# Attention in half sequences of 384 tokens, interleaved with the expert MLP, with zero-padded two-head matmuls

## The chip, the cores and the metric

The kernel runs on one core of a Trainium2 chip. Times are device microseconds (us), medians of several executions.

Engines: PE is the matmul array and PEld its weight loads, DVE the vector engine, ACT the scalar engine, POOL the GpSimd engine, SP the sync engine that issues loads and stores.

## The reference

Four batches, 8 heads, 768 tokens, head size 64. Attention is causal and linear, with a decay `lam` per head, and a running state per head. Its output is the input of an MLP with an ELU between two matmuls.

```python
for b in range(nb):                      # blocks of 64 tokens, in order
    intra = (qb @ kb.T * Dmask) @ vb     # Dmask = lam ** (i - j), causal
    inter = (qb * lam_pow) @ kv_state
    out[:, :, sl] = intra + inter
    kv_state = lam_block * kv_state + (kb * rev_pow).T @ vb
...
x = out.transpose(0, 2, 1, 3).reshape(3072, 512)
h = x @ w_in                             # 512 -> 2048
g = where(h > 0, h, exp(min(h, 0)) - 1)
return g @ w_out                         # 2048 -> 512
```

## The kernel before

It works in chunks of 128 tokens and pairs of heads. The whole attention comes first, then the whole MLP; the attention's buffers are closed in between. A head has 64 channels, so most attention matmuls use half of the 128x128 array: 64 rows (scores) or 64 columns (state update, output).

```python
def emit_A(gi, cp):                       # state update, scores, mask
    for dc in range(2):
        c = 2 * cp + dc
        for hh in range(2):
            ps = slice(hh * 64, (hh + 1) * 64)
            nc.tensor.matmul(psU[ps, c * 64 : (c + 1) * 64],
                lhsT=kd[:, hh, c, :], rhs=vn[:, hh, c, :], start=True, stop=True)
    ...
    nc.tensor.matmul(psSa[:, dc * 128 : (dc + 1) * 128],
        lhsT=qkt[0:64, c, 1, :], rhs=qkt[0:64, c, 0, :], start=True, stop=True)
    nc.tensor.matmul(psSb[:, dc * 128 : (dc + 1) * 128],
        lhsT=qkt[64:128, c, 1, :], rhs=qkt[64:128, c, 0, :], start=True, stop=True)
...
for si, (gi, cp) in enumerate(stages):    # attention, all of it
    ...
asb_cm.__exit__(None, None, None)
aps_cm.__exit__(None, None, None)
...
for mt in range(NMT):                     # then the MLP: 6 tiles of 512 tokens
    ...
    for n in range(NFT):                  # NFT = 16
        emit_mm1(n)                       # 4 matmuls of 512 columns, Exp, Relu, combine
        if n >= MLAG:
            emit_mm2(n - MLAG)            # 4 matmuls of 512 columns
    ...
    for ms in range(4):                   # eviction and store
        nc.vector.tensor_copy(osb[:], psM[ms][:])
```

Of the kernel before, what the change touches and what calls it, by code (L numbers as in the profile page):

```python
# [15 lines left out]
def kernel(  # L17
# [9 lines left out]
):  # L27
    nc = tc.nc
# [3 lines left out]
    NCH = S // L  # L32
    NST = NCH // 2
    NHP = H // 2
    NTOK = B * S
# [3 lines left out]
    MT = 512  # L39
    NMT = NTOK // MT  # L40
    MLAG = 3

    cpool = ctx.enter_context(tc.tile_pool(name="cst", bufs=1))
    xpool = ctx.enter_context(tc.tile_pool(name="xt", bufs=1))
    wpool = ctx.enter_context(tc.tile_pool(name="w", bufs=1))

    lam_b = cpool.tile([128, H], FP32, name="lam_b")
    nc.sync.dma_start(out=lam_b[:], in_=lam.unsqueeze(0).broadcast_to([128, H]))
    loglam = cpool.tile([128, H], FP32, name="loglam")
    nc.scalar.activation(loglam[:], lam_b[:], AF.Ln)  # L50

# [12 lines left out]
    caus2 = causT[:].unsqueeze(1).broadcast_to([128, 2, 128])  # L64

    iota_i = cpool.tile([128, 1], I32, name="iota_i")
    nc.gpsimd.iota(iota_i[:], pattern=[[0, 1]], base=0, channel_multiplier=1)
    in4 = cpool.tile([128, 4], FP32, name="in4")
    nc.vector.tensor_copy(in4[:, 0:1], iota_i[:])
    nc.vector.tensor_scalar_mul(in4[:, 1:2], in4[:, 0:1], -1.0)  # L70
    nc.vector.tensor_scalar(
        out=in4[:, 2:3], in0=in4[:, 0:1], scalar1=-1.0, scalar2=float(L),
        op0=ALU.mult, op1=ALU.add,
    )
    nc.vector.memset(in4[:, 3:4], float(L))
    pows = []
    for h in range(H):
        pw = cpool.tile([128, 4], FP32, name=f"pow{h}")
        nc.scalar.activation(pw[:], in4[:], AF.Exp, scale=loglam[:, h : h + 1])  # L79
        pows.append(pw)  # L80
    lamLp = cpool.tile([128, NHP], FP32, name="lamLp")
    for hp in range(NHP):
        h0, h1 = 2 * hp, 2 * hp + 1
        nc.vector.tensor_copy(lamLp[0:64, hp : hp + 1], pows[h0][0:64, 3:4])  # L84
        nc.vector.tensor_copy(lamLp[64:128, hp : hp + 1], pows[h1][64:128, 3:4])

    xt = [
        xpool.tile([128, NTOK], FP16, name=f"xt{hp}", tag=f"xt{hp}")
        for hp in range(NHP)
    ]  # L90

    w_in16 = [
        wpool.tile([128, DFF], FP16, name=f"wi16_{kk}", tag=f"wi16_{kk}")
        for kk in range(NHP)
    ]
    w_out16 = [
        wpool.tile([128, DM], FP16, name=f"wo16_{n}", tag=f"wo16_{n}")
        for n in range(NFT)
    ]
    w_jobs = [(w_in16[kk], moe_w_in[kk * 128 : (kk + 1) * 128, :]) for kk in range(NHP)]  # L100
    w_jobs += [(w_out16[n], moe_w_out[n * 128 : (n + 1) * 128, :]) for n in range(NFT)]
    w_sched = {}
    for j in range(NHP):
        w_sched[4 + 3 * j] = j
    for j in range(NFT):
        w_sched[15 + j] = NHP + j

    asb_cm = tc.tile_pool(name="asb", bufs=3)
    aps_cm = tc.tile_pool(name="aps", bufs=1, space=bass.MemoryType.PSUM)
    asb = asb_cm.__enter__()  # L110
    aps = aps_cm.__enter__()

    groups = [(b, hp) for b in range(B) for hp in range(NHP)]
    NG = len(groups)
    stages = [(gi, cp) for gi in range(NG) for cp in range(NST)]
    NSTAGE = len(stages)

    gqn = [None] * NG
    gkn = [None] * NG
    gvn = [None] * NG  # L120
    gqp = [None] * NG
    gkp = [None] * NG
    gkd = [None] * NG
    gqkt = [None] * NG
    gpsU = [None] * NG
    gP = {}
    kvs_cur = [None] * NG
    state_after = {}

    def emit_group_dma(gi):  # L130
        b, hp = groups[gi]
        h0 = 2 * hp
        qn = asb.tile([128, 2, NCH, 64], FP16, tag="qn", name=f"qn{gi}")
        kn = asb.tile([128, 2, NCH, 64], FP16, tag="kn", name=f"kn{gi}")
        vn = asb.tile([128, 2, NCH, 64], FP16, tag="vn", name=f"vn{gi}")
        nc.gpsimd.dma_start(
            out=qn[:], in_=q[b, h0 : h0 + 2].rearrange("h (c p) d -> p h c d", p=128)
        )
        nc.gpsimd.dma_start(
            out=kn[:], in_=k[b, h0 : h0 + 2].rearrange("h (c p) d -> p h c d", p=128)  # L140
        )
        nc.gpsimd.dma_start(  # L142
            out=vn[:], in_=v[b, h0 : h0 + 2].rearrange("h (c p) d -> p h c d", p=128)
        )
        gqn[gi], gkn[gi], gvn[gi] = qn, kn, vn

    def emit_group_prep(gi):
        b, hp = groups[gi]
        h0 = 2 * hp
        qn, kn = gqn[gi], gkn[gi]  # L150
        qp = asb.tile([128, NCH, 2, 64], FP16, tag="qp", name=f"qp{gi}")
        kp = asb.tile([128, NCH, 2, 64], FP16, tag="kp", name=f"kp{gi}")
        kd = asb.tile([128, 2, NCH, 64], FP16, tag="kd", name=f"kd{gi}")
        for hh in range(2):
            nc.vector.tensor_scalar_mul(qp[:, :, hh, :], qn[:, hh], pows[h0 + hh][:, 0:1])  # L155
            nc.vector.tensor_scalar_mul(kp[:, :, hh, :], kn[:, hh], pows[h0 + hh][:, 1:2])
            nc.scalar.activation(
                kd[:, hh], kn[:, hh], AF.Copy, scale=pows[h0 + hh][:, 2:3]
            )
        gqp[gi], gkp[gi], gkd[gi] = qp, kp, kd  # L160
        gqkt[gi] = asb.tile([128, NCH, 2, 128], FP16, tag="qkt", name=f"qkt{gi}")

    def emit_transposes(gi, cp):
        qp, kp, qkt = gqp[gi], gkp[gi], gqkt[gi]
        psT = aps.tile([128, 2, 2, 128], FP16, tag="psT", bufs=2, name=f"psT{gi}_{cp}")
        for dc in range(2):
            c = 2 * cp + dc
            nc.tensor.transpose(psT[:, dc, 0, :], in_=qp[:, c], identity=ident16[:])  # L168
            nc.tensor.transpose(psT[:, dc, 1, :], in_=kp[:, c], identity=ident16[:])
        nc.scalar.copy(out=qkt[:, 2 * cp : 2 * cp + 2, :, :], in_=psT[:])  # L170

    def emit_A(gi, cp):
        b, hp = groups[gi]
        qkt, vn, kd = gqkt[gi], gvn[gi], gkd[gi]
        if cp == 0:
            gpsU[gi] = aps.tile(
                [128, NCH * 64], FP32, tag="psU", bufs=2, name=f"psU{gi}"
            )
        psU = gpsU[gi]
        for dc in range(2):  # L180
            c = 2 * cp + dc
            for hh in range(2):
                ps = slice(hh * 64, (hh + 1) * 64)
                nc.tensor.matmul(
                    psU[ps, c * 64 : (c + 1) * 64],
                    lhsT=kd[:, hh, c, :], rhs=vn[:, hh, c, :], start=True, stop=True,
                )
        psSa = aps.tile([128, 256], FP32, tag="psSa", bufs=1, name=f"psSa{gi}_{cp}")
        psSb = aps.tile([128, 256], FP32, tag="psSb", bufs=1, name=f"psSb{gi}_{cp}")
        for dc in range(2):  # L190
            c = 2 * cp + dc
            nc.tensor.matmul(
                psSa[:, dc * 128 : (dc + 1) * 128],
                lhsT=qkt[0:64, c, 1, :], rhs=qkt[0:64, c, 0, :],
                start=True, stop=True,
            )
            nc.tensor.matmul(
                psSb[:, dc * 128 : (dc + 1) * 128],
                lhsT=qkt[64:128, c, 1, :], rhs=qkt[64:128, c, 0, :],
                start=True, stop=True,  # L200
            )
        P = asb.tile([128, 2, 2, 128], FP16, tag="pp", name=f"pp{gi}_{cp}")
        nc.vector.tensor_tensor(out=P[:, 0], in0=psSa[:], in1=caus2, op=ALU.mult)
        nc.vector.tensor_tensor(out=P[:, 1], in0=psSb[:], in1=caus2, op=ALU.mult)
        gP[(gi, cp)] = P
        for dc in range(2):
            c = 2 * cp + dc
            kvn = asb.tile([128, 64], FP16, tag="kvs", name=f"kvs{gi}_{c}")
            if c == 0:
                nc.vector.tensor_copy(kvn[:], psU[:, 0:64])  # L210
            else:
                nc.vector.scalar_tensor_tensor(
                    out=kvn[:], in0=kvs_cur[gi][:], scalar=lamLp[:, hp : hp + 1],
                    in1=psU[:, c * 64 : (c + 1) * 64], op0=ALU.mult, op1=ALU.add,
                )
            kvs_cur[gi] = kvn
            state_after[(gi, c)] = kvn

    def emit_B(gi, cp):
        b, hp = groups[gi]  # L220
        qkt, vn = gqkt[gi], gvn[gi]
        P = gP.pop((gi, cp))
        for dc in range(2):
            c = 2 * cp + dc
            psO = aps.tile([128, 128], FP32, tag="psO", bufs=2, name=f"psO{gi}_{c}")
# [22 lines left out]
    for si, (gi, cp) in enumerate(stages):  # L248
# [5 lines left out]
        if si + 1 < NSTAGE:  # L254
            ngi, ncp = stages[si + 1]
            if ncp == 0:
                emit_group_prep(ngi)
# [88 lines left out]
```

## Time and profile before

Median 300.47 us (299.87 to 301.43). The page's busy row shows PE at 9 tenths in nearly every slice, which hides two very different stages. The view by windows below gives busy microseconds of each engine in each stretch, the number of instructions in brackets.

```profile
core 0: us, PE busy (x) PEld busy (x) DVE busy (x) ACT busy (x) POOL busy (x), PEclk, DMA share, GB/s
0.00:7.30 7.30, 0.00 (x0) 0.00 (x0) 2.21 (x15) 4.39 (x11) 6.66 (x15) 1.00 1.07 68
7.30:124.50 117.20, 116.09 (x928) 64.54 (x929) 75.65 (x254) 66.08 (x175) 54.22 (x63) 1.00 1.42 113
124.50:128.50 4.00, 3.64 (x9) 1.36 (x10) 0.57 (x1) 1.38 (x4) 0.00 (x0) 1.00 0.00 0
128.50:292.70 164.20, 164.12 (x760) 74.18 (x758) 79.01 (x118) 101.39 (x190) 0.00 (x0) 1.00 0.09 33
292.70:298.10 5.40, 0.00 (x0) 0.00 (x0) 1.80 (x4) 0.00 (x0) 0.00 (x0) 0.79 0.51 194
```

| stage | us |
|---|---|
| first loads | 7.3 |
| attention alone | 117.2 |
| MLP alone (768 matmuls of 512 columns) | 168.2 |
| last evictions and stores | 5.4 |

How to read "busy PE": bars of matmuls overlap (the first ones below last 0.31 us each and start 0.105 us apart). What counts is the distance from start to start. The timeline of before (start, duration, engine, line, operation, output<-inputs, and in brackets the idle time before it with what ended it) shows two such distances for equal work:

```profile
118.74 0.31 PE L169 MATMUL psT_2_2004<-ident_68,kp_1924 128*128 128x128 f16 x1
118.85 0.31 PE L168 MATMUL psT_2_2004<-ident_68,qp_1923 128*128 128x128 f16 x1
118.95 0.31 PE L169 MATMUL psT_2_2004<-ident_68,kp_1924 128*128 128x128 f16 x1
...
119.92 0.18 PEld L229 LDWEIGHTS <-vn_1736 128*64 128x64 f16 x2 [0.20 <-issue]
...
120.27 0.13 PEld L237 LDWEIGHTS <-kvs_0_2000 64*64 64x64 f16 x2 [0.17 <-issue]
...
125.24 0.63 PE L281 MATMUL psH_0_2090<-xt_109,wi_1_113 128*128 128x512 f16 x1
125.67 0.63 PE L281 MATMUL psH_0_2090<-xt_110,wi_2_114 128*128 128x512 f16 x1
...
203.11 0.38 PE L299 MATMUL psM_2_2600<-wo_10_126,g_10_2749 128*128 128x512 f16 x1
203.32 0.38 PE L299 MATMUL psM_3_2601<-wo_10_126,g_10_2749 128*128 128x512 f16 x1
```

The first MLP matmuls, right after attention, start 0.43 us apart, the later ones 0.216 us. So attention ran at half of the rate that came later: 128-column matmuls at 0.105 us each. The granted clock (PEclk) reads 1.00 all the same: that column does not show this halving here. Where the array's shape changes, mostly 0.11 to 0.20 us pass before the weight load, marked "issue". The MLP stage itself has no gaps: 768 x 0.216 = 166 us.

### The profile page before, as it was taken

Reading aid. Unit: us, or ns where it says so; the run is one execution under the profiler, and the core shown is the slowest. Engines: PE = TensorE matmul, PEld = TensorE weight load, DVE = VectorE, ACT = ScalarE, POOL = GpSimd, SP = SyncE. Lnnn points to the kernel's source line nnn. Section 1 sums busy time; section 2 is a strip of 40 time slices with the busy share of each in tenths; the row PEclk is TensorE's granted clock in tenths of the full one; section 3 lists DMA queues with packets and bytes.
Section 4 is the critical chain, followed back from the end, with each engine's and each line's share of the span. In section 5 each row is a group of like instructions: output and inputs, shape, how many; then the busy total and the mean of one; then the engine's idle time right before and its main releaser. Section 6 shows DMA issues by size and latency. Waiting matters only on the chain.

```text
span 298.1 us, 4647 instructions
## 1 busy us (share of the span) xinstructions
PE 283.9 (95%) x1696; PEld 140.1 (47%) x1696; DVE 159.2 (53%) x388; ACT 173.2 (58%) x379; POOL 60.9 (20%) x77
## 2 busy tenths in 40 slices
PE   0999999999999999999999999999999999999992
PEld 0455555555555555444444444444444444444440
DVE  3666566777766566443455446443743563365343
ACT  6655555555555565276647665655656376647660
POOL 9744446666644410000000000000000000000000
PEclk9999999999999999999999999999999999999998
DMA  9999999999999940000012003000300030030003
GB/s 70 152 151 162 143 160 152 141 131 133 143 123 79 81 27 2 0 0 3 0 53 90 0 0 142 2 0 0 141 2 0 11 131 2 1 122 21 0 0 141
DMA packets 80998, 20.22 MB, mean 68 GB/s; under 512 B 75344, under 2 KB 77392, under 8 KB 80976
## 3 DMA queue, kind: packets, MB, share of 16 engines
q0 software_dynamic: 77376, 13.64, 58.4%
q1 hardware_dynamic: 3600, 6.30, 5.6%
q8 instruction: 13, 0.21, 0.3%
q14 instruction: 9, 0.07, 0.1%
HBM read 27.27 MB, written 6.29 MB: 113 GB/s over the span
## 4 chain that ended last, share of the span: by engine, by line
PE 93%; DVE 3%; ACT 1%; DMA 1%; issue 1%; DVEq 0%
PE psM_3_3369 L299 1%; PE psM_1_3367 L299 1%; PE psM_3_3113 L299 1%; PE psM_1_3111 L299 1%; PE psM_3_2857 L299 1%; PE psM_1_2855 L299 1%; PE psM_2_2344 L299 1%; PE psM_0_2342 L299 1%; PE psM_2_2088 L299 1%; PE psM_0_2086 L299 1%; PE psM_2_2600 L299 1%; PE psM_0_2598 L299 1%; PE psM_3_2601 L299 1%; PE psM_1_2599 L299 1%; PE psM_2_3368 L299 1%; PE psM_0_3110 L299 1%
## 5 line engine op out<-in xcount | busy, mean ns | idle before, releaser
L281 PEld LDWEIGHTS <-wi_1_113 128*128 128x128 f16 x96 | 9.5, 99 | 11.8 <-issue 0.8
L281 PEld LDWEIGHTS <-wi_2_114 128*128 128x128 f16 x96 | 9.5, 99 | 11.8 <-issue 0.8
L281 PEld LDWEIGHTS <-wi_0_112 128*128 128x128 f16 x96 | 9.5, 99 | 11.7 <-issue 0.7
L281 PEld LDWEIGHTS <-wi_3_115 128*128 128x128 f16 x96 | 9.5, 99 | 11.7 <-issue 0.6
L168 PE MATMUL psT_0_160<-ident_68,qp_150 128*128 128x128 f16 x2 | 0.6, 302 | 7.3 <-DVE qp_150 L155 7.3
L168 PEld LDWEIGHTS <-qp_150 128*128 128x128 f16 x6 | 0.6, 125 | 7.5 <-DVE qp_150 L155 7.3
L291 DVE SCALAR_TENSOR_TENSOR g_0_2099<-e_0_2095,r_0_2097 128x512 f16<-128x512 f32 x1 | 0.7, 691 | 3.6 <-ACT r_0_2097 L289 3.6
L287 ACT ACTIVATE e_0_2351<-psH_0_2346 128x512 f32<-128x512 f32 x1 | 0.6, 597 | 3.2 <-PE psH_0_2346 L281 3.2
L287 ACT ACTIVATE e_0_2607<-psH_0_2602 128x512 f32<-128x512 f32 x1 | 0.6, 597 | 3.2 <-PE psH_0_2602 L281 3.2
L287 ACT ACTIVATE e_0_3119<-psH_0_3114 128x512 f32<-128x512 f32 x1 | 0.6, 597 | 3.2 <-PE psH_0_3114 L281 3.2
L287 ACT ACTIVATE e_0_2863<-psH_0_2858 128x512 f32<-128x512 f32 x1 | 0.6, 597 | 3.2 <-PE psH_0_2858 L281 3.2
L287 ACT ACTIVATE e_0_3375<-psH_0_3370 128x512 f32<-128x512 f32 x1 | 0.6, 597 | 3.2 <-PE psH_0_3370 L281 3.2
L142 POOL DMA_DIRECT2D vn_1736<-in_v_dram x1 | 1.0, 1014 | 4.3 <-PE psO_5_1752 L237 4.3
L142 POOL DMA_DIRECT2D vn_1616<-in_v_dram x1 | 1.0, 1014 | 4.2 <-PE psO_5_1632 L229 4.2
L142 POOL DMA_DIRECT2D vn_518<-in_v_dram x1 | 1.0, 1014 | 4.0 <-PE psO_5_534 L237 4.0
L142 POOL DMA_DIRECT2D vn_276<-in_v_dram x1 | 1.0, 1014 | 3.8 <-PE psO_5_292 L229 3.8
L142 POOL DMA_DIRECT2D vn_639<-in_v_dram x1 | 1.0, 1023 | 3.7 <-PE psO_5_655 L229 3.7
L287 ACT ACTIVATE e_0_2095<-psH_0_2090 128x512 f32<-128x512 f32 x1 | 0.6, 597 | 2.0 <-PE psH_0_2090 L281 2.0
L50 ACT ACT_TABLE_LOAD x1 | 1.3, 1283 | 0.8 <-PEq L330 0.8
L229 PEld LDWEIGHTS <-vn_1736 128*64 128x64 f16 x12 | 1.3, 140 | 1.0 <-issue 0.4
L84 DVE COPY lamLp<-pow_83 64x1 f32<-64x1 f32 x1 | 0.1, 146 | 3.0 <-ACT pow_83 L79 3.0
L142 POOL DMA_DIRECT2D vn_1496<-in_v_dram x1 | 1.0, 1014 | 3.5 <-PE psO_5_1512 L229 3.5
(2250 smaller groups left out, 1023.5 us busy)
## 6 DMA issues: line engine op xcount, KB each, us to landing
wi_0_112<-in_moe_w_in_dram POOLq DMA_DIRECT2D x1, 512.0 KB, 7.8
wi_1_113<-in_moe_w_in_dram POOLq DMA_DIRECT2D x1, 512.0 KB, 7.0
wi_2_114<-in_moe_w_in_dram POOLq DMA_DIRECT2D x1, 512.0 KB, 6.8
wi_3_115<-in_moe_w_in_dram POOLq DMA_DIRECT2D x1, 512.0 KB, 6.2
out_dram<-osb_0_2330 SPq DMA_DIRECT2D x1, 256.0 KB, 2.1
out_dram<-osb_1_2333 SPq DMA_DIRECT2D x1, 256.0 KB, 2.2
out_dram<-osb_2_2336 SPq DMA_DIRECT2D x1, 256.0 KB, 2.2
out_dram<-osb_3_2339 SPq DMA_DIRECT2D x1, 256.0 KB, 2.3
```

Of the source, the lines that this page charges most:

```text
L50: nc.scalar.activation(loglam[:], lam_b[:], AF.Ln)
L84: nc.vector.tensor_copy(lamLp[0:64, hp : hp + 1], pows[h0][0:64, 3:4])
L142: nc.gpsimd.dma_start(out=vn[:], in_=v[b, h0 : h0 + 2].rearrange("h (c p) d -> p h c d", p=128))
L168: nc.tensor.transpose(psT[:, dc, 0, :], in_=qp[:, c], identity=ident16[:])
L229: nc.tensor.matmul(psO[ps, :], lhsT=vn[:, hh, c, :], rhs=P[:, hh, dc, :], start=True, stop=first, skip_group_check=True,)
L281: nc.tensor.matmul(psH[:], lhsT=w_in16[kk][:, n * 128 : (n + 1) * 128], rhs=xt[kk][:, m0 : m0 + MT], start=(kk == 0), stop=(kk == NHP - 1),)
L287: nc.scalar.activation(e[:], psH[:], AF.Exp)
L291: nc.vector.scalar_tensor_tensor(out=g[:], in0=e[:], scalar=-1.0, in1=r[:], op0=ALU.add, op1=ALU.min)
L299: nc.tensor.matmul(psM[ms][:], lhsT=g[:, ms * 128 : (ms + 1) * 128], rhs=w_out16[n][:], start=(n == 0), stop=(n == NFT - 1),)
```

## The change

The intent is to hide attention under the MLP. The MLP is cut into 8 tiles of 384 tokens (half a sequence), each 16 slots. A slot does the first layer of one slice of 128 hidden units (4 matmuls of 384 columns), then a piece of attention for a later tile, then the second layer of the slot two before (3 matmuls of 512 columns). Only the first tile's three chunks of attention run ahead of the MLP. Each attention matmul uses the full array: keys, values and states of two heads are held side by side with zeros in the other head's place. Decay moves from q and k into the mask and into the output scaling. Loads come per chunk, and weights in five slices.

```diff
+    CPT = 3
+    MT = CPT * L                     # 384 tokens
+    LAG = 2
+    ctx.enter_context(tc.manual_schedule())
...
+    for hh in range(2):
+        nc.sync.dma_start(out=lam_p[hh * 64 : (hh + 1) * 64, :],
+            in_=lam[hh::2].unsqueeze(0).broadcast_to([64, NHP]))
+    for c in range(NCB):             # first sequence: fp32, sync queue
+        for dst, src in zip(raw0, (q, k, v)):
+            nc.sync.dma_start(out=dst[:, c], in_=src[0, :, c * L : (c + 1) * L]...)
...
+    for i in range(2):               # zero padding
+        nc.gpsimd.memset(kz[i][64:128, :, 0, :], 0.0)
+        nc.gpsimd.memset(kz[i][0:64, :, 1, :], 0.0)
...
+    def att_SU(g, hp):               # scores and state update of two heads
+        for hh in range(2):
+            nc.tensor.matmul(pu[:, hh * 128 : (hh + 1) * 128],
+                lhsT=z[:, hp, hh, :], rhs=qt[:, hp, :], start=True, stop=True)
+        if not last:
+            nc.tensor.matmul(pu[:, 256:384]...,
+                lhsT=kds[g][:, 2 * hp : 2 * hp + 2, :], rhs=vz[:, hp, 0::2, :], ...)
+        nc.vector.tensor_tensor(out=P[:], in0=pu[:, 0:256]..., in1=mask[...], op=ALU.mult)
+        # two state updates of 64x64 on DVE
...
+    def F(g):                        # first slot of a chunk's attention
+        t, c = divmod(g, CPT)
+        if t == 1:
+            return 3 + 3 * c
+        return (t - 1) * NFT - 2 + 5 * c
...
+    for s in range(NMT * NFT + LAG):
+        if live:
+            er = mm1(s)              # first layer, Exp and Relu on ACT
+        for fn in slot_ops.get(s, []):
+            fn()                     # attention of a later tile
+        if live:
+            elu(s, *er)              # combine on DVE
+        if s >= LAG:
+            mm2(s - LAG)             # second layer; after n = 15 three evictions on DVE
```

Within a chunk, `att_T` (8 transposes) and `att_ev` (3 evictions on ACT) fall in slot F; `att_SU` of head pair hp in slot F+2+hp; `att_PI` (the output sums) one slot later; `att_X` (output scaling) in slot F+6. The scores (psSU) and the output sums (psO) have one memory bank each once the MLP runs.

## The prediction

> **What bounds the kernel now.** The sliced busy row shows PE at 9 tenths almost throughout, but the timeline splits it: (1) 0 to 7.3 us, PE waits for first loads and decay powers; (2) 7.3 to 124.5 us, attention alone, 117 us; (3) 124.5 to 292.7 us, the MLP, 768 matmuls of 512 columns; (4) 5.4 us of evictions and stores. In part 3 warm matmuls start 0.216 us apart: 768 x 0.216 = 166 us, no gaps, nothing to gain.
>
> Part 2 is inefficient for two reasons. First, 128-column transposes start 0.105 us apart, and the first MLP matmuls (125 to 128 us) 0.43 us apart, then 0.216. So attention ran at half array rate, although the granted-clock row says 9 tenths. [...] Second, between half-array matmuls (64 rows or columns) and full ones the timeline repeatedly shows 0.17 to 0.24 us "issue" idle before the weight load. [...]
>
> **The change.** The MLP runs as 8 tiles x 16 slots. A slot is 4 matmuls of 384 columns (0.162 us, scaled) and 3 of 512: 1.30 us; 128 slots = 166 us, unchanged. Attention is 24 chunks of 128 tokens, each at most 32 full-array 128-column matmuls, no mode changes. Three chunks precede the MLP; 21 (644 matmuls) are spread into slots[...]. Half of 0.105 is 0.053 us if weight loads hide; I expect 0.055 to 0.08, so 36 to 52 us in place of about 117.
>
> Other engines, from back-to-back distances of before: Exp and Relu 0.50 us, about 0.39 at 384 columns; transpose eviction 0.50, three a chunk; ELU combine about 0.47; mask product 0.34, four; eight state updates at 0.2; key and output scaling about 0.6 each. Five slots with a chunk: ACT 5.4 us, DVE 6.7, PE 8.3 to 9.1. PE remains the bound.
>
> **Critical path, estimated.**
> - Start, three chunks alone: constants to 7 us, then casts, transposes, evictions, about 5 us of DVE a chunk: first MLP matmul at 27 us (before: 125).
> - Cold MLP start: 2.
> - MLP 166, interleaved attention 43.
> - Tile boundaries: three single-buffered accumulator banks wait for 0.6 us evictions: 0.8 x 7 = 5.
> - First tile: chunks every 3 slots, with casts, and weight slices just in time (13 MB of early loads at the roughly 280 GB/s of before's q/k/v need 45 us): 4 lost.
> - Tail: 5.
> Predicted 252 us, range 239 to 270. Chances: faster by over 2% 0.96, same 0.03, slower 0.01.
>
> **Right or wrong in the profile.** First MLP matmul at 24 to 32 us; 384-column spacing near 0.162 us; 128-column spacing 0.055 to 0.08; no 0.2 us "issue" gaps; DVE under 85% in the steady middle; PE waits of 0.5 to 1 us on accumulator evictions at tile boundaries; few PE waits on weight DMA.
>
> **What would make it wrong.** 256-byte-run fp32 loads on the sync queue may land slowly, pushing the start past 32 us; weight slices may stall the first tile by 10 us or more; 128-column weight loads may not hide (each 0.01 us is 6.4 us); DVE or ACT order inside a slot may delay the combine that the second matmul needs two slots later[...]. Faster: start at 22 us and hidden weight loads give about 240.

Sum: 27 + 2 + 166 + 43 + 5 + 4 + 5 = 252 us. That 128-column matmuls would take half of 0.105 us inside the MLP is the author's estimate from the two rates of before, 0.43 and 0.216 us for 512 columns. The 2 us for a cold start fit before as well: its first nine MLP matmuls took 3.78 us from start to start, 1.8 more than at 0.216 us each. In this and the other texts "cold" and "slow clock" stand for the slow rate, "warm" and "doubled clock" for the fast one.

## The result, and the profile after

Median 271.15 us (269.87 to 272.00), before 300.46 us on the same chip. The ratio is 0.902, 95% interval 0.898 to 0.905: faster by 10%. Ratios here are the mean time of one kernel's fast runs over that of the other's fast runs of the same rounds, so not quite the ratio of the medians quoted. Executions over 1.5% slower than the fastest of the same kernel are left out of the means. The measured time lies 19 us above the predicted 252 and 1 us outside the range.

The view by windows of after, cut at the first MLP matmul, the ends of the first and seventh tile, and the last matmul:

```profile
core 0: us, PE busy (x) PEld busy (x) DVE busy (x) ACT busy (x) POOL busy (x), PEclk, DMA share, GB/s
0.00:31.40 31.40, 12.01 (x92) 9.47 (x93) 16.94 (x48) 12.96 (x26) 17.57 (x42) 1.00 1.03 152
31.40:72.40 41.00, 30.67 (x206) 16.97 (x205) 21.79 (x52) 23.12 (x50) 15.80 (x20) 0.96 1.42 157
72.40:238.50 166.10, 158.58 (x1217) 96.46 (x1218) 140.41 (x339) 109.44 (x245) 40.07 (x50) 1.00 0.54 59
238.50:262.70 24.20, 22.64 (x119) 11.26 (x116) 11.47 (x21) 14.25 (x33) 0.00 (x0) 1.00 0.09 34
262.70:268.10 5.40, 0.11 (x1) 0.00 (x0) 1.60 (x3) 0.00 (x0) 0.00 (x0) 0.92 0.40 147
```

PE is busy 95% of tiles 1 to 6, but only 75% of the first tile, which does about the same work in 41 us in place of 27.7. Below, the terms of the predicted sum are set against the same stretches of the profile; a tile is taken from its first first-layer matmul to that of the next tile, the last one to the end of the last matmul. A predicted tile is 166/8 for the MLP plus, where attention is interleaved, 43/7, plus 0.7 to 0.8 at its boundary.

| stretch | predicted | measured | off by |
|---|---|---|---|
| start, to the first MLP matmul | 27 | 31.4 | +4.4 |
| first tile (with slow start 2, loads 4) | 32.9 | 41.0 | +8.1 |
| tiles 1 to 6 | 165.6 | 165.9 | +0.3 |
| last tile | 21.5 | 24.4 | +2.9 |
| tail | 5 | 5.3 | +0.3 |
| timed median less the profile's span | 0 | 3.0 | +3.0 |

The pieces of the steady tiles, from the timeline of after (x4 is four instructions merged):

```profile
16.71 0.63 PE L218 MATMUL psT_241<-ident_118,qn_234 128*128 128x128 f16 x4
...
95.06 0.81 PE L312 MATMUL psH_1188<-xt_622,wi_4_108 128*128 128x384 f16 x4
...
95.83 0.22 PE L289 MATMUL psO_1140<-qT_1080,st_0_160 128*128 128x128 f16 x1
95.88 0.28 PE L242 MATMUL psSU_3_1200<-qT_1080,kz_154 128*128 128x128 f16 x2
95.99 0.22 PE L248 MATMUL psSU_3_1200<-v_2_150,kd_1084 128*128 128x128 f16 x1
96.05 0.38 PE L338 MATMUL psM_0_909<-wo_3_112,g_1152 128*128 128x512 f16 x1
...
97.51 0.39 PE L218 MATMUL psT_1226<-ident_118,qn_882 128*128 128x128 f16 x4
```

At 95.83, 95.88 (two), 95.99 and 96.05 us the 128-column matmuls start 0.055 us apart, with no gap towards the MLP matmul. Four transposes take 0.63 us ahead of the MLP and 0.39 us inside it: less the length of one (0.31 and 0.22), 0.107 against 0.057 us each. The same instruction in the same kernel is twice as fast among dense MLP work.

At each tile boundary the slot in which the second layer of the new tile begins takes 3.1 to 3.4 us, where a slot like it takes 1.5 to 1.6. The timeline of after at one of the seven boundaries, PE and the evictions alone:

```profile
103.83 0.56 DVE L324 SCALAR_TENSOR_TENSOR g_1303<-e_1287,r_1289 128x384 f16<-128x384 f32 x1
...
104.42 0.69 DVE L345 COPY osb_0_1308<-psM_0_909 128x512 f32<-128x512 f32 x1
105.03 0.68 DVE L345 COPY osb_1_1311<-psM_1_910 128x512 f32<-128x512 f32 x1
...
105.16 0.38 PE L338 MATMUL psM_0_1345<-wo_0_109,g_1277 128*128 128x512 f16 x1 [0.86 <-DVE osb_0_1308 L345]
...
105.76 0.38 PE L338 MATMUL psM_1_1346<-wo_0_109,g_1277 128*128 128x512 f16 x1 [0.22 <-DVE osb_1_1311 L345]
```

The three accumulators have one bank each. Their evictions begin only after the state updates and the combine that stand ahead of them in DVE's queue, and then take 0.6 us each.

In the first tile the view of waits on PE (waiting operation, what it waited for, us in total, times, longest) lists:

```profile
PE psH_577 L312 <- DMA wi_3_107<-in_moe_w_in_dram: 2.1, 1, 2.1
PE psT_440 L218 <- ACT qn_435 L188: 1.5, 1, 1.5
PE psSU_0_704 L242 <- DVE st_1_163 L268: 1.3, 1, 1.3
PE psT_524 L218 <- ACT qn_519 L188: 1.2, 1, 1.2
PE psSU_0_597 L242 <- DVE st_0_162 L268: 1.1, 1, 1.1
...
PE psO_735 L282 <- DVE xt_622 L298: 0.8, 1, 0.8
...
```

Two causes can be read here: late data (a weight slice, and the casts of chunks 3 to 5), and two chunks meeting in one bank (psSU waiting for the other chunk's state update, psO for its output scaling). A new chunk starts every 3 slots in this tile, but takes 4 slots for its scores and as many for its sums. Besides, after such waits the slow rate came back: near 53 us three 512-column matmuls start 0.43 us apart, in place of 0.216, and four 384-column matmuls take 1.49 us, in place of 0.81. The granted clock reads 0.51 from 52.1 to 55.2 us. The longest wait of PE in this tile before that was 2.1 us, with shorter ones beside it.

At the start, the loads ahead of the first query chunk stand out. The view of one tile (lam_p, the decay factors) in after has:

```profile
  DMA lam_p<-in_lam_dram: 5.2, 1
...
DMA to landing us min/median/max: 5.6/6.1/6.7
```

The two loads of 1 KB each, issued at 1.2 and 2.0 us, land at 6.8 and 8.7 us, 3.5 and 1.9 us behind the load ahead of each. ACT sits idle for 5.2 us on them, and the first query chunk, behind them in the sync queue, lands at 9.9 us; the following 256 KB loads land 1.1 to 1.2 us apart up to 17.9 us. The last fp32 chunk and the last weight slice land at 60 us.

### The profile page after: what moved, and what is told of

Same layout as the page of the kernel before. It is cut to its first block, busy times and chain, and to the rows that moved or that the text cites. A ratio compares the mean times of both kernels' runs of the same rounds, so it can differ in the third digit from the quotient of the medians.

```text
span 268.1 us, 4675 instructions
## 1 busy us (share of the span) xinstructions
PE 224.0 (84%) x1632; PEld 134.2 (50%) x1632; DVE 192.2 (72%) x461; ACT 159.8 (60%) x351; POOL 73.4 (27%) x111
## 4 chain that ended last, share of the span: by engine, by line
PE 63%; SPq 15%; DVE 8%; DMA 7%; issue 4%; ACT 1%; DVEq 0%; ACTq 0%
SPq L74 14%; DMA raw_v<-in_v_dram 7%; PE psM_2_2205 L338 1%; PE psM_2_3057 L338 1%; PE psM_2_2627 L338 1%; PE psM_2_1769 L338 1%; PE psM_2_911 L338 1%; PE psM_2_1347 L338 1%; PE psM_0_1767 L338 1%; PE psM_0_1345 L338 1%; PE psM_0_2625 L338 1%; PE psM_0_2203 L338 1%; PE psM_0_909 L338 1%; PE psM_1_1346 L338 1%; PE psM_1_2204 L338 1%
## 5 line engine op out<-in xcount | busy, mean ns | idle before, releaser
L312 PEld LDWEIGHTS <-wi_3_107 128*128 128x128 f16 x128 | 12.7, 100 | 14.5 <-DMA wi_3_107<-in_moe_w_in_dram 2.5
L312 PEld LDWEIGHTS <-wi_2_106 128*128 128x128 f16 x128 | 12.5, 98 | 11.7
L312 PEld LDWEIGHTS <-wi_4_108 128*128 128x128 f16 x128 | 12.5, 98 | 11.7
L218 PE MATMUL psT_187<-ident_118,qn_182 128*128 128x128 f16 x4 | 0.6, 308 | 12.6 <-ACT qn_182 L188 12.6
L312 PEld LDWEIGHTS <-wi_1_105 128*128 128x128 f16 x64 | 6.4, 100 | 8.9 <-issue 4.2
L242 PEld LDWEIGHTS <-kz_154 128*128 128x128 f16 x96 | 8.3, 105 | 4.9 <-POOL kd_200 L201 1.5
L181 POOL DMA_DIRECT2D v_3_151<-in_v_dram x6 | 4.5, 753 | 22.4 <-PE psO_2149 L289 8.7
L312 PEld LDWEIGHTS <-wi_0_104 128*128 128x128 f16 x64 | 6.5, 103 | 7.5 <-issue 2.0
L242 PEld LDWEIGHTS <-kz_155 128*128 128x128 f16 x96 | 8.0, 101 | 3.5 <-issue 1.4
L181 POOL DMA_DIRECT2D v_0_148<-in_v_dram x6 | 4.5, 757 | 15.6 <-PE psO_1715 L282 8.4
L181 POOL DMA_DIRECT2D v_1_149<-in_v_dram x6 | 4.5, 750 | 13.5 <-PE psO_1003 L289 5.0
L181 POOL DMA_DIRECT2D v_4_152<-in_v_dram x6 | 4.5, 755 | 12.4 <-PE psO_1441 L289 5.0
L181 POOL DMA_DIRECT2D v_5_153<-in_v_dram x6 | 4.5, 756 | 11.7 <-PE psO_2431 L289 4.3
L181 POOL DMA_DIRECT2D v_2_150<-in_v_dram x6 | 4.5, 757 | 9.3 <-PE psO_1140 L289 4.6
L141 DVE TENSOR_TENSOR mask<-causT,dn 128x1024 f32<-128x1024 f32 x1 | 1.2, 1224 | 7.8 <-ACT dn L130 7.8
L218 PEld LDWEIGHTS <-qn_182 128*128 128x128 f16 x4 | 0.3, 130 | 12.6 <-ACT qn_182 L188 12.6
L282 PEld LDWEIGHTS <-v_2_150 128*128 128x128 f16 x32 | 3.4, 106 | 3.4 <-issue 1.9
L282 PEld LDWEIGHTS <-v_4_152 128*128 128x128 f16 x32 | 3.2, 99 | 3.7 <-issue 1.8
L282 PEld LDWEIGHTS <-v_1_149 128*128 128x128 f16 x32 | 3.4, 108 | 2.6 <-issue 1.0
L282 PEld LDWEIGHTS <-v_5_153 128*128 128x128 f16 x32 | 3.1, 98 | 2.8 <-issue 0.9
L282 PEld LDWEIGHTS <-v_0_148 128*128 128x128 f16 x32 | 3.2, 108 | 2.3 <-issue 0.6
```

Of the source, the lines that this page charges most:

```text
L141: nc.vector.tensor_tensor(out=mask[:], in0=causT[:].unsqueeze(1).broadcast_to([128, H, 128]), in1=dn[:].unsqueeze(2).broadcast_to([128, H, ...
L181: nc.gpsimd.dma_start(out=vz[:, :, 2 * hh, :], in_=v[b, hh::2, rows].rearrange("h p d -> p h d"))
L218: nc.tensor.transpose(pt[:, 0, hp, :], in_=qn[:, 2 * hp : 2 * hp + 2, :], identity=ident16[:])
L242: nc.tensor.matmul(pu[:, hh * 128 : (hh + 1) * 128], lhsT=z[:, hp, hh, :], rhs=qt[:, hp, :], start=True, stop=True,)
L282: nc.tensor.matmul(po[:, hp, :], lhsT=vz[:, hp, hh : hh + 2, :], rhs=P[:, hh, :], start=(hh == 0), stop=(hh == 1 and cb == 0), skip_group_ ...
L312: nc.tensor.matmul(pH[:], lhsT=wi[:, kk, j * 128 : (j + 1) * 128], rhs=xt[m][:, kk, :], start=(kk == 0), stop=(kk == NHP - 1),)
```

## The experiments

Each kernel is an edit of after unless it says otherwise, and was timed in three rounds against before. "First tile" and "start" are read from the trace as in the table above. Tiles 1 to 7 came out within 0.1 us of those of after in every run that did not touch them. The first tile is less steady: each figure is one execution, in E8 it is 1.9 us longer than in after although the edit does not touch it, and the profiled execution of after is its fastest. So differences of under 2 us in the first tile are not read as an effect.

| run | edit | time | start | first tile | tiles 1 to 6 | last tile |
|---|---|---|---|---|---|---|
| after | | 271.15 | 31.4 | 41.0 | 165.9 | 24.4 |
| E1 | chunk every 4 slots | 268.96 | 31.1 | 40.4 | 165.9 | 24.4 |
| E2 | no loads of chunks 3 to 5 | 263.91 | 31.1 | 35.4 | 165.9 | 24.4 |
| E3 | weights ahead of prefetches | 271.68 | 31.1 | 43.9 | 165.9 | 24.4 |
| E4 | no strided decay loads | 264.52 | 29.1 | 38.4 | 165.9 | 24.4 |
| E5 | second layer held back a slot | 277.92 | 31.3 | 42.9 | 173.5 | 23.8 |
| E6 | half-array state update | 280.88 | 31.6 | 43.8 | 174.7 | 24.4 |
| E7 | casting loads for chunks 3 to 5 | 262.45 | 31.3 | 33.6 | 165.9 | 24.4 |
| E8 | evictions on ACT | 260.84 | 31.1 | 42.9 | 156.4 | 23.5 |
| B1 | E4 + E7 + E8 | 249.73 | 29.3 | 33.2 | 156.4 | 23.5 |
| B2 | B1 + E1 | 245.07 | 29.8 | 28.1 | 156.4 | 23.5 |
| B3 | all chunks by casting loads | 239.76 | 24.6 | 28.0 | 156.4 | 23.5 |
| E9 | no interleaving | 325.67 | 139.5 | 20.6 | 135.2 | 24.4 |

### E1: one chunk every 4 slots in the first tile

```diff
-            return 3 + 3 * c
+            return 1 + 4 * c
```

> Only the slots of chunks 3 to 5 change: one chunk every 4 slots (1, 5, 9) in place of every 3 (3, 6, 9), so that no slot holds two chunks' score matmuls or two chunks' output sums. Theory crowding (two chunks fight over one score bank and one output bank): the four PE waits of 0.8 to 1.3 us on state updates and output scaling in the first tile go, the first tile falls from 41 to about 36 us, the time from 271 to about 267. Theory loads (fp32 loads and weights arrive late): those waits turn into waits on loads or casts and the time stays within 1 us of 271.

268.96 us, and 40.4 us for the first tile. The waits on the other chunk's bank went down to 0.7 us, those on psO for the output scaling went away, and waits on the casts and on a mask product behind them came in their place (2.0 us the longest). Taken alone the edit gains 2 us in time, and in the profiled first tile 0.6 us, which is within its unsteadiness: nearer to the theory of late loads, without ruling out crowding, because the late loads could hide it. B2 settles that.

### E2: no loads of chunks 3 to 5 (wrong result)

```diff
-    for c in range(NCB):
+    for c in range(CPT):
         for dst, src in zip(raw0, (q, k, v)):
...
+        rc = c % CPT
...
-        nc.scalar.copy(qn[:], qf[:, c])
+        nc.scalar.copy(qn[:], qf[:, rc])          # the same for kn and v
```

> Wrong result on purpose: the fp32 loads of chunks 3 to 5 are not made, and their casts read chunks 0 to 2 again; every other instruction stays. Theory loads: the weight wait of 2 us, the wait for the last value chunk and the cold clock that follows go, the first tile falls from 41 to 34 us or less, the time to 264 or less. Theory crowding: the four bank waits stay, the first tile falls by 3 us at most, time 268 or more.

263.91 us; the first tile falls by 5.6 us to 35.4. The weight wait is gone from PE's list. The bank waits (2.2 and 1.6 us) stay, and so do 2.6 us of waits on the casts, with their data long there: those are the casts' own place in ACT's queue. So late loads cost 5 to 6 us, and they are not the whole loss.

### E3: weights ahead of the prefetches

```diff
-    loads += [(4 * i - 4, lambda i=i: emit_w_load(i)) ...]
+    loads += [(-1, lambda i=i: emit_w_load(i)) ...]
```

> The five weight slices are queued ahead of the later chunks' prefetches on the Pool queue; nothing else changes. Theory loads, by order: the wait on weight slice 3 (2 us) and the cold clock after it go, 267 to 268 us. Theory loads, by sheer volume of the sync queue's fp32 traffic: the weights come no earlier by more than a microsecond and the time stays at 270 to 271. Theory crowding: 270 to 271.

271.68 us, no gain; the profiled first tile got longer (43.9 us). The wait on weights is gone, but the fp32 chunks now come later: PE waits 2.4 us for chunk 3's key scaling, which stands in DVE's queue behind the cast of that chunk's values (landed at 42.9 us, in after at 30.8), and 1.9 us for the cast of chunk 4's keys (landed at 49.8 us, in after at 41.2). Reordering moved the wait, as the theory of sheer volume says. By 60 us the core had loaded, in after, 4.7 MB of fp32 chunks, 8.4 MB of weights and about 1.6 MB of prefetches, 14.7 MB in 57 us or about 260 GB/s (worked out from sizes and landing times).

### E4: the decay factors without the two strided loads

```diff
-    for hh in range(2):
-        nc.sync.dma_start(out=lam_p[hh * 64 : (hh + 1) * 64, :],
-            in_=lam[hh::2].unsqueeze(0).broadcast_to([64, NHP]))
...
+        nc.vector.tensor_copy(lam_p[hs, :], lam_b[hs, hh::2])    # for both halves
```

> The two small strided loads of the decay factors ahead of the data loads are replaced by two tiny copies from the factors already on the chip. In the trace of after they take until 8.7 us to land and the first data load lands 1.2 us behind them, at 9.9. Theory start (these two loads hold up the sync queue and the decay constants, and everything up to the first MLP matmul shifts with them): first query chunk at about 5 us, first MLP matmul at 27 in place of 31.4, and, since the first tile then still waits for DMA volume, the time 267 to 269. Rival (the vector engine's work on three chunks alone sets the start): first MLP matmul at 30 or later, time 270 to 271.

264.52 us. The first query chunk landed at 4.9 us in place of 9.9, as expected. The first MLP matmul came only at 29.1 us in place of the expected 27, because one of the two tiny copies (4 columns) took 2.8 us on DVE and held up the constants until 6.7 us. POOL was filling tiles with zeros at the time, in fills of at most 0.52 us each. In B3, where DVE does the fills, the slower of the two copies took 0.63 us (in B1 and B2, with the fills on POOL, 2.8 us again), but no run isolates the cause. The first tile was 2.6 us shorter as well, all loads behind having come earlier; that is little more than its unsteadiness.

### E5: the second layer of a new tile held back by one slot

```diff
-            mm2(s - LAG)
+            n = (s - LAG) % NFT
+            if s - LAG < NFT or n > 1:
+                mm2(s - LAG)
+            elif n == 1:
+                mm2(s - LAG - 1)
+                mm2(s - LAG)
```

> The first second-layer matmuls of a tile are held back by one slot, so that the evictions of the tile before run beside another first-layer group. Theory boundary (the slot at each tile boundary takes 3.2 us in place of 1.5 because three single-buffered banks are evicted one by one behind other vector work): 1.0 to 1.5 us less at each of seven boundaries, time 261 to 264. Rival (the wait only moves, to the score bank or to the first layer's two banks): under 3 us gained.

277.92 us: slower by 7 us, a clear miss of my own theory. Only the last tile, which carries no attention, gained (23.8 against 24.4 us). The timeline of E5 at a boundary:

```profile
106.60 1.89 DVE L345 COPY osb<-psM 128x512 f32<-128x512 f32 x3
...
108.41 0.41 DVE L254 TENSOR_TENSOR pp<-psSU,mask 128x256 f16<-128x256 f32 x1
...
108.87 0.27 PE L282 MATMUL psO<-pp,v 128*128 128x128 f16 x2 [1.74 <-DVE pp L254]
...
112.06 1.48 PE L312 MATMUL psH<-xt,wi 128*128 128x384 f16 x4
```

PE no longer waits for the accumulators. It now waits 1.74 us for the next mask product, which stands behind 1.9 us of evictions in DVE's queue. By 112 us the matmuls are at the slow rate (four of 384 columns in 1.48 us, against 0.81). So the boundary costs DVE time in DVE's order; moving the consumer does not help.

### E6: the state update in the half-array form

```diff
-            nc.tensor.matmul(pu[:, 256:384]..., lhsT=kds[g][:, 2 * hp : 2 * hp + 2, :],
-                rhs=vz[:, hp, 0::2, :], start=True, stop=True)
+            for hh in range(2):
+                nc.tensor.matmul(
+                    pu[hh * 64 : (hh + 1) * 64, 256 + hh * 64 : 256 + (hh + 1) * 64],
+                    lhsT=kds[g][:, 2 * hp + hh, :], rhs=vz[:, hp, 2 * hh, :], start=True, stop=True)
```

> Only the state-update matmul is turned back into the half-array form of before: two matmuls with 64 columns of the array each, in place of one full one; same result. Theory tile-mode (each change between half and full array leaves the array idle for about 0.2 us, as in before): two changes per head pair, eight per chunk, 18 chunks with an update in the interleaved part, so 20 to 29 us more, 290 to 300 us, with idle gaps of 0.15 to 0.24 us marked issue before these weight loads. Rival (the gaps in before came from its slow clock and dependences, not from the mode): within 3 us of 271.

280.88 us, 9.7 us slower: the direction of the tile-mode theory, at less than half of its size. The timeline of E6, to be held against the lines at 95.88 to 96.05 us of after:

```profile
117.84 0.28 PE L242 MATMUL psSU<-qT,kz 128*128 128x128 f16 x2
...
118.05 0.22 PE L249 MATMUL psSU<-v,kd 128*64 128x64 f16 x2
...
118.20 0.82 PE L339 MATMUL psM<-wo,g 128*128 128x512 f16 x3
```

From the first score matmul to the first MLP matmul behind the update it is 0.36 us, where after needs 0.17. A slot with an update takes 1.7 us in place of 1.5. I had taken 0.2 us for each change of form, as in before; at the fast rate it is about 0.2 us for going to the half array and back. The extra matmul of the pair is not what costs: the two half matmuls start 0.003 us apart, and the time goes before them and after them (0.15 us each from start to start, in place of 0.056). Part of the loss is absorbed at the boundaries.

### E7: casting loads for chunks 3 to 5

```diff
-    for c in range(NCB):
+    for c in range(CPT):
         for dst, src in zip(raw0, (q, k, v)):
...
-        evs.append((f, lambda g=g: (emit_cast_first(g) if g < NCB else None, att_T(g), ...
+        evs.append((f, lambda g=g: (att_T(g), ...
-    for g in range(NCB, NG):
-        loads.append((F(g) - 12, lambda g=g: emit_load(g)))
+    for g in range(CPT, NG):
+        loads.append((F(g) - 12 if g >= NCB else 4 * (g - CPT) - 0.5, lambda g=g: emit_load(g)))
```

> Chunks 3 to 5 are loaded by the casting loads of the Pool queue, as the later chunks are, between the weight slices, and are not cast on the scalar and vector engines. Theory DMA volume (the first 60 us move some 15 MB at about 270 GB/s and the first tile waits for that): the bytes read stay, but a casting load of 256-byte runs moved about 280 GB/s in before against about 225 here on the sync queue, so 1 to 3 us gained, 268 to 270. Theory casts (the three chunks' casts on the scalar engine hold up the transposes): the waits of 1.2 to 1.5 us on them go and 3 to 4 us are gained, 267 to 268.

262.45 us (three fast executions, 262.3 to 264.8); the first tile of the profiled one falls by 7.4 us to 33.6. That is more than either theory gave. In PE's waits of the first tile the waits on casts are gone and that on weights is down to 0.7 us; what is left are the bank waits (2.4 and 1.6 us). The edit cures both the late loads and the casts' place in ACT's queue, so it does not split the two; E2 does, at 5.6 us for the loads. The loads' rates, worked out from landing times: 256 KB on the sync queue every 1.1 to 1.2 us in after, until the weights join at 18 us (about 230 GB/s), a casting load of 384 KB of fp32 on the POOL queue every 1.4 us in before (about 280 GB/s).

### E8: evictions on the scalar engine

```diff
-                nc.vector.tensor_copy(o[:], psM[m][i][:])
+                nc.scalar.copy(o[:], psM[m][i][:])
```

> The three output accumulators of a tile are evicted by the scalar engine in place of the vector engine. Theory boundary order (the evictions stand in the vector engine's queue behind the state updates and the combine, and the mask product of the next slot stands behind them): the slot at the boundary falls from 3.2 to about 2.0 us, seven times, time 262 to 264. Rival (the scalar engine then delays the next exponentials as much as it helps): less than 3 us gained.

260.84 us, the largest single gain. The slot at the boundary falls from 3.1 to 3.4 us to 1.7 to 1.9, better than expected (at the last boundary to 2.2), and PE's waits on the accumulators fall from up to 0.86 us to at most 0.14 us each. ACT starts the evictions right behind its Relu, 0.1 us after the first accumulator's last matmul has ended; in after DVE began them 1.5 us behind that matmul:

```profile
103.26 1.57 ACT L345 COPY osb<-psM 128x512 f32<-128x512 f32 x3
...
104.41 0.84 PE L338 MATMUL psM<-wo,g 128*128 128x512 f16 x3
104.68 0.55 ACT L317 ACTIVATE e<-psH 128x384 f32<-128x384 f32 x1
```

These lines of E8 show the three evictions as one stretch on ACT, the three second-layer matmuls of the new tile as one stretch, and the next Exp following. The profiled first tile was 1.9 us longer than in after; there PE waited 3.3 us for a weight slice, so waits for loads vary from run to run.

### B1, B2, B3: the mends together

> Three mends together: no small strided loads of the decay factors, chunks 3 to 5 by the casting loads, evictions on the scalar engine. If the three losses are separate terms, their single gains of about 6, 7.5 and 10 us add up, less what the first two share in the first tile (both shorten its waits for loads, about 3 us): 250 to 252 us. If they overlap more, 253 to 256.

B1: 249.73 us. The single gains (6.6, 8.7 and 10.3 us) add up to 25.6; 21.4 came. The missing 4.2 us are near the 3 us that E4 and E7 were expected to share in the first tile; the fast executions of E7 alone differ by 2.5 us.

> The three mends and one chunk every 4 slots in the first tile in place of every 3. Theory crowding, second form (its waits on the score and output banks are real, but late loads hid them when it was tried alone): with the loads mended the first tile falls by 3 to 4 us against the three mends alone. Rival (loads still bind there): within 1 us of the three mends.

B2 differs from B1 in the one line of E1. 245.07 us: 4.7 us less, and 5.1 us less in the first tile. The waits on the two banks in B1's first tile:

```profile
PE psSU L240 <- DVE st L266: 2.5, 3, 1.3
PE psO L280 <- DVE xt L296: 1.6, 2, 0.9
```

In B2 these lines shrink to one, and nothing else is left beside the wait at the tile's own start:

```profile
PE psSU L240 <- DVE st L266: 0.2, 1, 0.2
```

So crowding was real and worth 5 us; in E1 late loads had hidden it.

> As the four mends, but all six first chunks come by casting loads, queued first on the Pool queue, with the zero fills moved to the vector engine, and the prefetches of later chunks behind more of the weights: no fp32 copies and no casts at all. Start: the constants end at about 7 us, and three chunks of 4.5 us vector work follow: first MLP matmul at 24 to 26 us; first tile about 30 us; time 243 to 248 us. If the vector engine's chain alone sets the start, no earlier than 27 us and 247 to 250.

B3 keeps the four mends and loads the first three chunks by casting loads as well, first in the POOL queue, with the zero fills on DVE and later prefetches moved behind more weights:

```diff
+    for g in range(CPT):
+        emit_load(g)                 # casting loads, right after the masks and iotas
+    emit_w_load(0)
+    emit_w_load(1)
...
-        nc.gpsimd.memset(...)        # all zero fills
+        nc.vector.memset(...)
-        eng = nc.gpsimd if g == 0 else nc.vector
+        eng = nc.vector              # scaling of the first keys
```

239.76 us (239.43 to 240.15), correct, ratio 0.797 to before (0.795 to 0.799): faster than both kernels, and below the expected range. First MLP matmul at 24.6 us. Loading all first chunks this way takes 5.2 us off the start against B2; the casts, the fills and the earlier landing are not separated.

### E9: the new attention without interleaving

All 24 chunks run ahead of the MLP, in the order that after uses for its first three.

```diff
-    for g in range(CPT):
-        emit_cast_first(g)
+    for g in range(NG):
+        if g < NCB:
+            emit_cast_first(g)
+        if g + 3 >= NCB and g + 3 < NG:
+            emit_load(g + 3)
...                                   # no attention in the slots; 8 buffers for xt;
                                      # scores of head pairs 0 to 2 always in the psM banks
```

> All 24 chunks of the new attention run before the MLP, in the order that after uses for its first three; no chunk is interleaved. Theory overlap (the gain comes from hiding attention under the MLP at the doubled clock): the vector engine needs about 4.8 us a chunk, so attention takes about 115 us by itself, as before, and the time is 290 to 305. Rival (the full-array form without tile-mode changes is faster by itself): attention alone takes 80 us or less, time 265 or less.

325.67 us, slower than before by 8%, and beyond the expected 290 to 305. The view by windows of E9 has attention from 12.6 to 139.5 us:

```profile
12.60:139.50 126.90, 76.12 (x736) 62.70 (x737) 103.57 (x303) 45.82 (x83) 67.14 (x83) 0.72 1.28 118
139.50:325.10 185.60, 170.88 (x899) 87.67 (x896) 85.94 (x153) 111.58 (x256) 0.00 (x0) 0.99 0.09 35
```

By itself the new attention takes 127 us, against 117 in before: DVE is busy 82% of it, PE only 60%. The first six chunks, fed by the fp32 loads, take 42.5 us of it (DVE idles up to 6.8 us for one load); the other 18 take 4.7 us each, as expected. So part of the excess over the expected time is late loads. The steady MLP tiles without attention take 22.5 us, against 27.7 with it. Three chunks thus cost 5.2 us inside the MLP, 1.74 us a chunk, and 14.1 us alone (3 x 4.7, once the loads no longer hold them up).

The array's rate in E9 is a surprise that none of the theories covers. Of the pairs of full-array 128-column matmuls that follow each other without a gap in this attention, 356 start about 0.107 us apart and 273 about 0.056 (34 between). Of 158 such pairs in the attention of before none came at the fast rate (120 at the slow one, 38 between), although PE was busy there 116 of 117 us. So the fast rate does not need the MLP, and a PE that is busy in the profile does not always get it. What kept before at the slow rate, its half-array matmuls for one, no run here isolates.

E9 also shows a tile boundary with no attention beside it:

```profile
185.71 0.56 DVE L324 SCALAR_TENSOR_TENSOR g<-e,r 128x384 f16<-128x384 f32 x1 [0.74 <-ACT r L319]
...
186.19 1.88 DVE L345 COPY osb<-psM 128x512 f32<-128x512 f32 x3
...
186.92 0.38 PE L338 MATMUL psM<-wo,g 128*128 128x512 f16 x1 [0.85 <-DVE osb L345]
```

Its slot takes 3.08 us against 1.30, the same loss of 1.8 us as with attention: the combine and the evictions' own length make it, and the state updates ahead of them add nothing to see.

## Why the prediction was right or wrong

**Right: the mechanism.** The gain comes from hiding attention under the MLP. E9 shows it: the same instructions without interleaving lose 25 us to before. Late loads do not explain that: its first six chunks took 14 us more than six later ones, and without these 14 us it would still be slower than before (an estimate, 325.7 - 14 = 312 us against 300.5). The forecast of 0.055 to 0.08 us for a 128-column matmul held at its lower end, 384-column matmuls came at 0.16 us, and the slots have no gaps of "issue". The trace shows the two rates (0.107 against 0.057 us for the transposes, ahead of the MLP and inside it), and interleaved attention got the fast one. What sets the rate is not shown: PE was busy 116 of 117 us at the slow rate in before's attention, and E9 reached the fast rate in part with PE busy 60%.

**Right in sum, by two errors that cancel: tiles 1 to 6.** Predicted 165.6, measured 165.9 us: luck. Interleaved attention was put at 43/7 = 6.1 us a tile and took 5.2. The tile boundary was put at 0.8 us and took about 1.75: three evictions of 0.6 us were counted as mostly overlapping the next first-layer group, but they stand in DVE's queue behind the combine (and the state updates, which by E9 do not matter), one after the other. The step "0.8 x 7 = 5" was mis-sized; it measured about 12 us, and E8 gave 10.3 us back. The last tile, with a boundary and no attention to cancel it, shows the error openly: 24.4 against 21.5.

**Wrong: "First tile: ... 4 lost".** The first tile took 41.0 us, 8.1 more than predicted. With loads and schedule mended (B2) it takes 28.1, so the loss was 13 us in all. About 7.4 us of it were the fp32 loads of chunks 3 to 5 and their casts (E7; E2 puts the loads alone at 5.6), and about 5 us were two chunks sharing one bank (B2 against B1). The prediction named the first as a risk ("weight slices may stall the first tile by 10 us or more") but counted 13 MB and left out the prefetches queued among the weights; and it saw the chunks "every 3 slots" without asking which banks two chunks would share. This step is the largest part of the miss, 8.1 of 19 us.

**Wrong: "first MLP matmul at 27 us".** It came at 31.4, inside the band of 24 to 32 but above the value in the sum. I took constants to be ready at 7 us. Two loads of 1 KB, of four-byte runs, held up the constants and the first data loads until 8.7 us. E4 takes them away: 2.3 us at the start and, in the profiled execution, 2.6 us in the first tile.

**Left out: 3.0 us** between the profile's span and the timed median, although the profile and the times of before already showed such a difference (2.4 us). In after 1.8 us of it lie between span and time of one and the same execution; the other 1.3 us are that the profiled execution was faster than the median.

Of the other tests named: DVE is busy 84.5% of tiles 1 to 6, just under the stated limit of 85%; PE waited on weights once, for 2.1 us; the waits on evictions come to about 1.3 us a boundary, where 0.5 to 1 was said.

What stays open: what kept the array at its slow rate in before's attention; how the casts, the zero fills and the landing times share the 5.2 us that B3 gains at the start; why one tiny copy of E4 took 2.8 us; and why waits on weights in the first tile differ by one or two microseconds between runs.

## What to carry to other kernels

When one stage leaves the array at its slow rate, hiding it inside a dense stage can gain more than running it by itself (here 271.15 us against 325.67 in E9; no run here tuned this attention alone), but the prologue and the first tile, where nothing hides yet, must be costed load by load: sum all bytes queued by then, prefetches too, and read which queue each waits in. For each slot of an interleaved schedule, list what stands ahead in the queue of every engine, and which single-buffered banks two overlapping pieces share; a wait like the 1.75 us at each tile boundary here shows there, not in busy shares. Try mends together before giving one up: E1 alone gained 2 us, and 5 once the loads no longer hid it.
